# The softmax shift taken from the first 8 keys of a head instead of the first 16

## The chip, the cores and the metric

The kernel runs on one core of a Trainium2 chip. The metric is the device time of one execution in microseconds (us); the time of a kernel is the median of its runs. One execution is also recorded by the hardware profiler, and the profile and the trace are of that one.

## What is computed

Two branches of the same input `x` (2048 tokens of 448) are mixed by a gate `g` per token. Branch A is attention with 16 heads of 28, whose heads share one set of keys and values. Branch B is a layer norm, a token shift and an MLP of width 1792.

```python
q = (x @ wq) -> 16 heads of 28;  k = x @ wk;  v = x @ wv      # one k and v for all heads
scores = einsum("bhqd,bkd->bhqk", q, k) * 28 ** -0.5
p = softmax(scores)                                            # over 2048 keys
a = einsum("bhqk,bkd->bhqd", p, v) -> 448 columns @ wo
hs = shift(gelu(layernorm(x) @ w1)) @ w2;  x1 = x + hs
b = x1 + gelu(layernorm(x1) @ w3) @ w4
out = g * a + (1 - g) * b
```

A softmax is the same for any shift that is subtracted from all scores of a query, as long as nothing overflows or vanishes.

## The kernel before

The work is in three stages, each in an order that is written out by hand for every engine (nothing is rescheduled). Matmuls of stages 1 and 2 are made in three products of a high and a low part each.

- Stage 1 (to about 125 us): queries, keys and values of all tokens (`proj`, L133 to L139), the first layer norm, `w1` (`h`), `w2` (`hs`).
- Stage 2 (to about 397 us): the MLP in four blocks of 512 tokens. Each block has 14 tiles `g`: 11 products with `w3` (L135 to L139, moving operands `ah` and `al`), two GELUs on ACT (L689, L690), the low part on DVE (L691), then 3 products with `w4` for each of 4 token tiles (L699 to L701). `w3` and `w4` come in seven sets `w3h`, `w3l`, `w4h`, `w4l`; the first three sets lie in one pool (`s2a`), the other four in another.
- Stage 3: attention, in 16 units. A unit `u` is 512 queries by 4 heads. It passes over 16 key tiles, two per iteration, so 8 iterations `i` per unit.

An iteration of stage 3 has, on PE, the scores of two key tiles (`scores`, L204; 4 heads side by side in 4 row strips), then the products with the values of the two key tiles of the iteration before (`values`, L893; 4 heads in 4 column strips, in two halves of 256 queries), and mostly one "job": a product with `wo` (L844). The trace shows each f32 product of L893 and L844 as two records. On ACT it has the exponentials (`exps`, L257). DVE copies a half of one key tile's scores out of its banks (L954), adds the values' products up (`values_end`, L818) and adds the job's result (L860).

The shift: subtracting it happens inside the score products, since two spare rows of the queries `qh` hold the negated shift and the same rows of the keys hold 1. It is an estimate, the maximum over the first `MK` keys. `khd` holds these keys in bf16, four times on a diagonal, so that one product gives all four heads at once: 32 queries, in one of 4 column strips, by `4 * MK` columns.

```python
for i, t in enumerate(ts):                       # max_products: 4 token tiles
    for c in range(4):                           # by 4 column strips
        ...
        nc.tensor.matmul(ps[32 * c:32 * c + 32, i * 4 * MK:(i + 1) * 4 * MK], q, khd,
                         start=True, stop=True, tile_position=(0, 32 * c))
...
nc.vector.reduce_max(mx_of[u][:, :, ts[0]:ts[0] + n].rearrange("p j t -> p t j"),     # max_reduce
                     ps[:, 0:n * 4 * MK].rearrange("p (t j k) -> p t j k", t=n, j=4), axis=AX.X)
```

`max_part` calls both (L211 and L218). For unit 0 this is done in stage 2, among the `w4` products. For every later unit it is done in the iteration `i == 2` of the unit before, between the two halves of the values' products, into a score bank that is free just then; the next iteration's scores write that bank again. One iteration later `max_end` (L246 to L254) negates the result, splits it into two parts, transposes it and sends it into the spare rows by DMA.

`khd` is filled on POOL in stage 2 (L734 clears it, L737 casts the keys in, four times). On POOL also stand the clears of a part of the weight sets `w3h` (L111, in stages 1 and 2).

Because the shift is only an estimate, the reciprocals of all sums are compared with `LIMIT = 1e18` and `1 / LIMIT` (`check`, L801). The flags are counted at the end (L1056, L1059); if one is not good, a general path follows (`redo`, from L1066): for all 16 units again, with `max_full`, the maximum over all keys.

Of the kernel before, what the change touches and what calls it, by code (L numbers as in the profile page):

```python
# [30 lines left out]
EPS = 1e-5  # L31
SHIFTS = (-1, 1, -2, 2)
PB = 5
MK = 16
LIMIT = 1e18


def f32(ap):
    return ap.bitcast(F32)
# [3 lines left out]
def gated_mix_kernel(  # L43
# [162 lines left out]
    def max_products(u, ts, ps):  # L206
        for i, t in enumerate(ts):
            for c in range(4):
                m = t * P + 32 * c
                q = f32(qh_of[u])[:, m:m + 32].bitcast(BF16).rearrange("p (m e) -> p m e", e=2)[:, :, 1]  # L210
                nc.tensor.matmul(ps[32 * c:32 * c + 32, i * 4 * MK:(i + 1) * 4 * MK], q, khd,  # L211
                                 start=True, stop=True, tile_position=(0, 32 * c))

    def max_reduce(u, ts, ps):
        if u not in mx_of:
            mx_of[u] = late.tile([P, 4, 4], F32, tag="mr", bufs=2, name=f"mr_{u}")
        n = len(ts)
        nc.vector.reduce_max(mx_of[u][:, :, ts[0]:ts[0] + n].rearrange("p j t -> p t j"),  # L218
                             ps[:, 0:n * 4 * MK].rearrange("p (t j k) -> p t j k", t=n, j=4), axis=AX.X)

# [41 lines left out]
    with tc.tile_pool(name="s1b", bufs=1) as s1b, \  # L262
# [325 lines left out]
        late = ctx.enter_context(tc.tile_pool(name="late", bufs=1, side="right", reuse_waits="tile"))  # L588
        khd = late.tile([P, 4 * MK], BF16, name="khd")
        kh_of.append(late.tile([P, S], F32R, name="kh"))  # L590
# [76 lines left out]
    with tc.tile_pool(name="s2", bufs=1, reuse_waits="tile") as s2, \  # L667
# [35 lines left out]
        for b in range(NB):  # L703
            acc = [ps2.tile([P, 512], F32, tag="acc", bufs=4, name=f"acc_{b}_{t}") for t in range(4)]
            gs = {}
            for f in range(NF):
# [26 lines left out]
                if b == 1 and f == 1:  # L733
                    nc.gpsimd.memset(khd, 0.0)  # L734
                    for j in range(4):
                        h = slice(32 * j, 32 * j + DH)
                        nc.gpsimd.tensor_copy(khd[h, j * MK:(j + 1) * MK], f32(kh_of[0])[h, 0:MK])  # L737
                    qr0 = s2a.tile([P, 512], F32, tag="xn", bufs=1, name="qr_0")
# [406 lines left out]
```

## Time and profile before

| | |
|---|---|
| median of 3 runs | 911.8 us (911.51 to 913.12) |
| the profiled execution | 911.48 us |
| its span, first to last instruction | 909.7 us |
| busy: PE, ACT, DVE, POOL | 903.1, 632.6, 515.8, 79.1 us |
| granted TensorE clock, mean | 0.999 |

In the profile PE is TensorE's matmuls and PEld its weight loads, which run beside the matmuls; DVE is VectorE, ACT ScalarE, POOL GpSimd and SP the engine that issues most DMAs. A row of a group reads: line, engine, operation, output <- inputs, output <- input shape, number | busy us, mean ns of one | idle time before it. A row of the timeline reads: start us, length us, engine, line, operation, and in brackets the idle time before it and what ended it. L12 is line 12 of the kernel.

### The profile page before, as it was taken

The numbers are of one execution on the slowest core, as the hardware profiler recorded it, in microseconds if no ns is written. First come the engines' busy times: TensorE is split into PE (matmuls) and PEld (weight loads), VectorE is DVE, ScalarE is ACT, GpSimd is POOL, SyncE is SP. The second block draws the span as 40 slices with busy tenths as digits, with TensorE's granted clock in tenths as the row PEclk, the third lists the DMA queues.
The fourth block names the chain that finished last, engine by engine and source line by source line (L and its number), as shares of the span: only waits on it lengthen the run. The fifth ranks groups of instructions, "written<-read, shape, count | busy, mean of one in ns | idle before, by whom it ended". The sixth has DMA issues, their size and how long they took to land.

```text
span 909.7 us, 24149 instructions
## 1 busy us (share of the span) xinstructions
PE 903.1 (99%) x10360; PEld 626.8 (69%) x10360; DVE 515.8 (57%) x960; ACT 632.6 (70%) x1003; POOL 79.1 (9%) x116
## 2 busy tenths in 40 slices
PE   9999999999999999999999999999999999999998
PEld 6788888888888888875555555555555555555554
DVE  3665273631441531136766777676767667767665
ACT  5542444332132231269999999999999999999995
POOL 3243320200000520020000000000000000000000
PEclk9999999999999999999999999999999999999999
DMA  8832653120110120010000001000011000010001
GB/s 294 289 103 61 147 167 129 37 70 1 39 49 2 22 65 1 1 52 24 14 25 14 24 15 56 23 25 17 25 33 36 24 14 25 15 55 14 15 14 44
DMA packets 40726, 47.31 MB, mean 52 GB/s; under 512 B 10152, under 2 KB 28904, under 8 KB 40616
## 3 DMA queue, kind: packets, MB, share of 16 engines
q1 hardware_dynamic: 37448, 40.43, 15.2%
q10 hardware_dynamic: 3168, 5.31, 1.6%
q8 instruction: 82, 1.34, 0.6%
q14 instruction: 28, 0.23, 0.1%
HBM read 32.56 MB, written 11.67 MB: 49 GB/s over the span
## 4 chain that ended last, share of the span: by engine, by line
PE 97%; ACT 2%; DMA 1%; DVE 0%; issue 0%; SPq 0%
PE bank L893 26%; PE bank L204 20%; PE bank L844 6%; PE acc L701 5%; PE acc L699 5%; PE acc L700 5%; PE g L135 4%; PE g L137 4%; PE g L136 4%; PE pair L204 2%; ACT p L257 2%; PE hs L475 1%; PE hs L476 1%; PE g L138 1%; PE g L139 1%; PE h L136 1%
## 5 line engine op out<-in xcount | busy, mean ns | idle before, releaser
L257 ACT ACTIVATE p<-bank 128x512 f32<-128x512 f32 x514 | 265.9, 605 | 4.4 <-POOL pick L866 1.5
L893 PE MATMUL bank<-p,vext 128*32 128x256 f32 x4064 | 247.7, 382 | 1.0 <-ACT p L257 1.0
L893 PEld LDWEIGHTS bank<-p,vext 128*32 128x32 f32 x4064 | 117.9, 110 | 115.9 <-ACT p L257 53.0
L954 DVE COPY p<-pair 128x1024 f32<-128x1024 f32 x125 | 153.0, 1224 | 57.9 <-PE pair L204 40.9
L689 ACT ACTIVATE gh<-g 128x512 fp32r<-128x512 f32 x55 | 32.9, 598 | 181.7 <-PE g L139 181.7
L818 DVE TENSOR_TENSOR o<-o,bank 128x256 f32<-128x256 f32 x222 | 93.5, 421 | 80.4 <-PE bank L893 72.3
L257 ACT ACTIVATE p<-p 128x1024 f32<-128x1024 f32 x126 | 138.0, 1096 | 0.0
L257 ACT ACTIVATE p<-pair 128x1024 f32<-128x1024 f32 x129 | 136.8, 1060 | 0.0
L691 DVE TENSOR_TENSOR gl<-gf,gh 128x512 fp32r<-128x512 f32 x55 | 38.6, 702 | 164.9 <-ACT gf L690 164.9
L204 PE MATMUL bank<-qh,kh 32*128 32x512 f32 x514 | 114.8, 443 | 0.0
L204 PE MATMUL pair<-qh,kh 32*128 32x512 f32 x510 | 114.0, 443 | 0.0
L204 PE MATMUL bank<-qh,kl 32*128 32x512 f32 x514 | 101.8, 389 | 0.0
L204 PE MATMUL bank<-ql,kh 32*128 32x512 f32 x514 | 101.6, 390 | 0.0
L204 PE MATMUL pair<-qh,kl 32*128 32x512 f32 x510 | 101.3, 389 | 0.0
L204 PE MATMUL pair<-ql,kh 32*128 32x512 f32 x510 | 100.9, 389 | 0.0
L204 PEld LDWEIGHTS bank<-qh,kh 32*128 32x128 f32 x514 | 48.0, 182 | 61.3 <-issue 38.7
L701 PE MATMUL acc<-w4h,gl 128*128 128x448 f32 x220 | 80.7, 367 | 0.0
L699 PE MATMUL acc<-w4h,gh 128*128 128x448 f32 x220 | 80.2, 364 | 0.0
L700 PE MATMUL acc<-w4l,gh 128*128 128x448 f32 x220 | 79.8, 363 | 0.0
L844 PE MATMUL bank<-wof,on 128*32 128x224 f32 (+1 forms) x984 | 69.6, 357 | 0.0
L135 PE MATMUL g<-ah,w3h 128*128 128x512 f32 x168 | 65.4, 389 | 0.0
L136 PE MATMUL g<-al,w3h 128*128 128x512 f32 x168 | 65.4, 389 | 0.0
(206 smaller groups left out, 1394.1 us busy)
## 6 DMA issues: line engine op xcount, KB each, us to landing
qd<-qf ACTq DMA_DIRECT2D x15, 256.0 KB
rb<-rd SPq DMA_DIRECT2D x15, 256.0 KB
x<-in_x_dram SPq DMA_DIRECT2D x4, 896.0 KB
xd<-xt SPq DMA_DIRECT2D x16, 224.0 KB
w34raw<-in_w_dram SPq DMA_DIRECT2D x7, 512.0 KB
qr<-qd SPq DMA_DIRECT2D x64, 56.0 KB
w34raw<-in_w_dram SPq DMA_DIRECT2D x7, 448.0 KB
out_dram<-ot SPq DMA_DIRECT2D x14, 224.0 KB
```

The source lines that it names most:

```text
L135: nc.tensor.matmul(ps, wh[:, c, :], ah[:, c, :], start=(c == 0), stop=False)
L136: nc.tensor.matmul(ps, wh[:, c, :], al[:, c, :], start=False, stop=False)
L204: nc.tensor.matmul(ps[j], k[h, keys], q[h, :], start=(r == 0), stop=(r == 2), tile_position=(32 * j, 0))
L257: nc.scalar.activation(p[:, heads], p[:, heads] if source is None else source, AF.Exp, scale=SCALE)
L691: nc.vector.tensor_sub(gl, gf, f32(gh))
L699: nc.tensor.matmul(ps, gh[:, tok], w4h[i][:, k, :], start=(f == 0), stop=False)
L700: nc.tensor.matmul(ps, gh[:, tok], w4l[i][:, k, :], start=False, stop=False)
L701: nc.tensor.matmul(ps, gl[:, tok], w4h[i][:, k, :], start=False, stop=(f == stop))
L818: nc.vector.tensor_add(o, o, pv)
L844: nc.tensor.matmul(ps[32 * i:32 * i + 32, :], a[:, c:c + 32], w, start=start, stop=stop, tile_position=(0, 32 * i))
L893: nc.tensor.matmul(pv[32 * j:32 * j + 32, :], vext[:, kt, :], p_of[k][:, j, qs], start=(k == ks[0]), stop=(k == ks[-1]), tile_position=(0, ...
L954: nc.vector.tensor_copy(pa[:, both], pairs[0])
```

## The change

One constant:

```diff
-MK = 16
+MK = 8
```

`khd` becomes 128x32 instead of 128x64, the products of L211 have 32 columns instead of 64, the reduction of L218 reads 128 elements per partition instead of 256 (16 groups of 8 instead of 16), and the casts of L737 take 8 keys instead of 16. The general path with all keys stays.

No instruction is added, removed or moved on any engine. On PE, at the `w4` products of stage 2 where the estimate for unit 0 stands (`m` is its PSUM tile, `acc` that of the `w4` products), the order reads, in part:

```order
 L701 MATMUL acc_0_2293<-w4h_1068,gl_0_2310 128x448
 L211 LDWEIGHTS qh_1048
-L211 MATMUL m_2354<-khd,qh_1048 32x64
+L211 MATMUL m_2354<-khd,qh_1048 32x32
 L211 LDWEIGHTS qh_1048
```

All 256 products change in this way, and each keeps its own load of weights. On POOL, at the clears of `w3h` at the end of stage 1 and at the filling of `khd` in stage 2, with the semaphores that each instruction waits for:

```order
 L111 MEMSET w3h_0_1066 64x256 [waits PE_49,Pool_49]
-L111 MEMSET w3h_1_1186 64x256 [waits PE_49]
+L111 MEMSET w3h_1_1186 64x256
 L111 MEMSET w3h_2_1229 64x256
 L111 MEMSET w3h_3_1295 64x256 [waits DMAHW5_49,DMAHW4_49,PE_49]
...
-L734 MEMSET khd_1046 128x64
-L737 CAST khd_1046<-kh_1047 28x16 [waits Pool_49]
+L734 MEMSET khd_1046 128x32
+L737 CAST khd_1046<-kh_1047 28x8 [waits Pool_49]
 L739 MEMSET qr_0_1848 128x512 [waits DVE_49,Pool_49]
```

The second clear no longer waits for PE: `khd` takes 64 bytes less per partition, the buffers that are allocated below it (the pools `bigs` and `s2a`: raw inputs, `ah`, `al`, the first three weight sets and small statistics tiles) lie 64 bytes higher, and one of them no longer touches a buffer of stage 1 that PE still reads. All other waits are the same.

## The prediction, made before the changed kernel ran

> **What bounds the kernel now.** I read the page first: the busy shares, then the chain that ended last.
>
> ```profile
> PE 903.1 (99%) x10360; PEld 626.8 (69%) x10360; DVE 515.8 (57%) x960; ACT 632.6 (70%) x1003; POOL 79.1 (9%) x116
> PE 97%; ACT 2%; DMA 1%; DVE 0%; issue 0%; SPq 0%
> ```
>
> TensorE is in use for nearly the whole span and carries 97% of the chain. The shares are averages, so next come the stages. The estimate of the maximum (products at L211, reduction at L218) is made once in stage 2 and fifteen times in stage 3. Two views of one line each, the instructions of L211 and those of L218:
>
> ```profile
> L211 PEld LDWEIGHTS <-qh x256: 91/97/98, 270.6 to 845.0; 128*32 128x32 bf16 x128
> L211 PE MATMUL pair<-khd,qh x240: 192/193/194, 408.1 to 845.1; 128*32 128x64 bf16 x120
> L211 PE MATMUL m<-khd,qh x16: 192/193/204, 270.6 to 270.7; 128*32 128x64 bf16 x16
> L218 DVE TENSOR_REDUCE mr<-pair x15: 418/421/421, 408.7 to 845.6; 128x16 f32<-128x256 f32 x15
> ```
>
> So there are 16 blocks of 16 products. Those of stage 3 lie one unit apart, about 31.2 us ((845.1 - 408.1) / 14), at 408, 439, 470 and so on to 845 us. In stage 3 two engines are nearly full, and it has to be told which sets the pace. The table by windows (columns: window, length, then busy us and instructions of PE, PEld, DVE, ACT, POOL, then clock and DMA), the waits of ACT from 445 to 880 us, and the head of the chain from 414 to 446 us:
>
> ```profile
> 445.00:900.00 455.00, 455.00 (x7678) 257.87 (x7673) 319.28 (x602) 451.76 (x697) 0.00 (x0) 1.00 0.08 24
> ACT p L257 <- PE pair L204: 0.4, 1, 0.4
> by line: ACT p L257 44.4%; PE bank L893 25.4%; PE bank L204 21.6%; PE bank L844 4.7%; issue 2.7%; PE pair L204 1.8%
> ```
>
> From 445 us PE has no gap at all, at full clock. ACT is close behind. Before 446 us, where iterations with and without an output job alternate, ACT is the largest part of the chain. The chain in order of time around one block (start, us, what) settles the later stretch:
>
> ```profile
> 465.14 1.91 PE bank L893 x32
> 467.05 0.38 PE bank L844 x8
> 467.43 0.42 PE bank L204
> ...
> 469.03 1.05 PE bank L893 x16
> 470.08 0.12 PE pair L211 x16
> 470.20 0.87 PE bank L893 x16
> 471.06 0.38 PE bank L844 x8
> 471.44 0.43 PE bank L204 x2
> ...
> 475.33 0.43 PE bank L204 x2
> ```
>
> Nothing but PE stands in it. From one start of the scores to the next it is 471.44 - 467.43 = 4.01 us with the block in between, and 475.33 - 471.44 = 3.89 us without. The difference, 0.12 us, is the block's own row. In this stretch the block is therefore paid in full, once per unit.
>
> **The change part by part.**
>
> *The products, 256 of them, from 64 columns to 32.* Their number, their weights and their place stay. Thirteen blocks (470 to 845 us) lie where PE paces, two (408 and 439 us) where ACT does, and one in stage 2. In the thirteen a block costs 0.12 us, that is 4 turns of the four column strips at 30 ns. Two things could set the 30 ns. If it is the columns that stream, half of them take half the time: 0.06 us saved per block. If it is the rate at which loads and products follow one another, nothing much is saved. The block of stage 2 shows that rate, since its 16 loads run without older work in front (timeline; start, us, engine, line):
>
> ```profile
> 270.33 0.37 PE L701 MATMUL acc<-w4h,gl 128*128 128x448 f32 x1
> 270.62 0.18 PEld L211 LDWEIGHTS <-qh 128*32 128x32 bf16 x16 [0.31 <-issue]
> 270.62 0.30 PE L211 MATMUL m<-khd,qh 128*32 128x64 bf16 x16
> 270.86 0.19 PEld L699 LDWEIGHTS acc<-w4h,gh 128*128 128x128 f32 x1
> ```
>
> Sixteen loads of 97 ns fit in 0.18 us, so one follows another after (180 - 97) / 15 = 5.5 ns; sixteen products of 193 ns fit in 0.30 us, which is (300 - 193) / 15 = 7.1 ns each. Sixteen pairs need 0.09 to 0.11 us at this rate, whatever their width, against the 0.12 us now. That leaves 0.01 to 0.03 us per block. I take 0.015 us, since the measured rate of the products (7.1 ns) is nearer to the block's own (120 / 16 = 7.5 ns) than to half of it. Thirteen blocks: 0.2 us; if the columns set it, 13 x 0.06 = 0.8 us; the whole block gone would be 13 x 0.12 = 1.6 us, a bound that nothing can reach while the loads stay.
>
> The Trainium skill speaks against the larger sum: TensorE: Matmul & The Clock Gate, section "Wait — 56ns, not 53.3ns?", says that start to start never drops below about 25 ns however few the columns are. Applied to each of the four turns of a block, that rule would leave an estimated 30 - 25 = 5 ns per turn, 0.02 us per block and 0.26 us for the thirteen. The trace shows no product of 32 columns, so it neither bears the floor out nor denies it; the 30 ns of a turn at 64 columns lie above it.
>
> In the two ACT-paced blocks PE has time to spare, so I count nothing; by the streaming price they would bring at most 2 x 0.06 us. The one of stage 2 stands on the path of a PE-paced stage too, with its first load exposed (0.31 us idle): 0.015 us by the issue rate, 0.06 us at most, and the exposed load stays.
>
> *The reduction, 16 times from 256 to 128 elements.* The nearest rows are the present one, 420 ns, and a narrow one on the same engine:
>
> ```profile
> L246 DVE TENSOR_SCALAR mc<-mr 128x16 fp32r<-128x16 f32 x13 | 2.1, 165 | 0.0
> 470.20 0.42 DVE L818 TENSOR_TENSOR o<-o,bank 128x256 f32<-128x256 f32 x1 [0.55 <-PE bank L893]
> 470.54 0.42 DVE L218 TENSOR_REDUCE mr<-pair 128x16 f32<-128x256 f32 x1
> 471.19 0.42 DVE L818 TENSOR_TENSOR o<-o,bank 128x256 f32<-128x256 f32 x1 [0.23 <-issue]
> ```
>
> (420 - 165) / 240 = 1.06 ns per element, so an estimated 0.14 us less each time and 2.2 us in all. I cost it at nothing, because the next L818 starts 0.23 us after the reduction has ended: it waits for the second half of L893 on PE, not for DVE. The next scores overwrite the reduced bank only at 471.44, half a microsecond after 470.96, with the job's products (0.38 us) between. In the two early blocks no job lies between, but there ACT paces. If that cover were gone, up to 0.14 us per block would come on top.
>
> *POOL: a narrower clear and four narrower casts of the key copy, and one wait less.* The timeline of POOL:
>
> ```profile
> 118.80 0.81 POOL L111 MEMSET w3h<- 64x256 f32 x3
> 124.88 0.82 POOL L111 MEMSET w3h<- 64x256 f32 x3 [5.27 <-PE hs L478]
> ...
> 171.36 0.16 POOL L734 MEMSET khd<- 128x64 bf16 x1
> 171.58 1.01 POOL L737 CAST khd<-kh 28x16 bf16<-28x16 f32 x4
> 176.78 0.53 POOL L739 MEMSET qr<- 128x512 f32 x1 [4.19 <-DVE xt L164]
> ```
>
> The wait that goes belongs to the second of the six clears, which ran inside the first three without a gap: it was met already. The 5.27 us belong to the fourth, whose wait stays. The casts, 1.01 us, end 4.19 us before POOL's next work can start, and their first reader comes at 270.6 us. Nothing to gain or lose.
>
> *A shift of addresses.* The key copy takes 64 bytes less per partition, so the allocator puts the buffers of stage 2 that lie below it 64 bytes higher: ah and al (moving in all w3 products), the first three of seven weight sets, and the raw buffers. The trace has no column for addresses; I bound the cost by rows whose tiles stand at both offsets. In the built program the tiles of stage 1 lie at offset 96 modulo 128, those of stage 2 at 32 before and at 96 (or still at 32) after. Groups by form, of 120 to 400 us and of 20 to 95 us:
>
> ```profile
> L135 PE MATMUL g<-ah,w3h 128*128 128x512 f32 x168 | 65.4, 389 | 0.0
> L135 PE MATMUL h<-ahk,w1h 128*112 128x512 f32 x36 | 14.2, 396 | 0.0
> L139 PE MATMUL q<-ahk,wql 128*128 128x512 f32 x10 | 3.9, 389 | 0.0
> ```
>
> At offset 96 the same product took 389 ns in one group and 396 in another, in a stage with more traffic. I take the 389, which is the quieter group with weights of the same width: no cost. The ends are nothing and 7 ns on each of 616 w3 products (56 sets of 11), 4.3 us.
>
> *The sum.* -0.2 us on a span of 909.7 us and a profiled execution of 911.48 us, so 909.5 and 911.3. The median of the runs shown is 911.8, 0.3 above the profiled one; the forecast for the median is 911.8 - 0.2 = 911.6 us. A change of 0.2%, 1.8 us, is about what a measurement of this kernel can tell from none, so this is the middle class.
>
> **The rivals.**
>
> *Faster: DVE turns out to pace the blocks.* If the release of the bank by L218 were what PE waits for, the 0.14 us of each of 15 reductions would come through beside the 0.06 us of the products: 15 x 0.2 = 3.0 us, 908.8 us. For it speaks that the early blocks have the next scores right behind the reduction; against it that PE shows no gap from 445 us. To pass 1.8 us it needs 0.12 us in every block. I give this, and other gains of that size, 0.12.
>
> *Slower: the moved buffers make the w3 products dearer.* Price 7 ns x 616 = 4.3 us by the row of 396 ns: 915.9 us. It decides from 1.8 / 616 = 3 ns a product on. For it: one group at the new offset is that slow, and stage 2 is PE-bound, so each ns counts. Against it: two groups at the two offsets both take 389 ns. 0.10.
>
> *Slower by far: the general path runs.* A shift from 8 keys is lower, so sums of exponentials grow; past 1e18 the kernel repeats the attention with a maximum over all keys. Worked out from the reference's inputs by the kernel's formula, the largest logarithm of a sum over the shift goes from 25.1 (16 keys) to 30.0 (8 keys), the least stays at 0.1; the limit is ln 1e18 = 41.4. Were it to run, the scores, exponentials and values alone would come again, at least 16 units x 8 iterations x 3.89 us = 498 us: over 1,400 us. 0.02.
>
> *The change doesn't act at all* (a block stays at 0.12 us): 911.8 us, inside the forecast's class, 0.3 of its 0.76.
>
> **How the numbers follow.** Forecast 0.76 (gain between 0 and 0.8 us), faster 0.12, slower 0.10 + 0.02 = 0.12. The range starts from 911.8 - 0.8 = 911.0 and from the spread of the runs, 911.51 to 913.12 (0.3 below the median, 1.3 above it). That gives 911.0 - 0.3 = 910.7 and 911.8 + 1.3 = 913.1; with some of both rivals, 910.4 to 913.2.
>
> **What would show it right or wrong.** Right: the L211 row of the chain between 0.09 and 0.12 us, 16 blocks as before, L218 near 0.28 us with the wait of L818 behind it longer by as much, 3.89 us per iteration, 389 ns for w3 products, and no instruction from the general path. Streaming would show as an L211 row of 0.06 us. Wrong: another mean for L135 to L139 or L699 to L701, ACT idle in stage 3, an iteration after a block that is shorter than 3.89 us, or instructions behind the last output's store.

## The result and the profile after

| | before | after |
|---|---|---|
| median of 16 runs each | 911.83 us (911.39 to 913.12) | 913.72 us (913.26 to 914.3) |
| the profiled execution | 911.48 us | 913.26 us |
| its span | 909.7 us | 911.4 us |

The changed kernel is slower: after over before is 1.0019, with a 95% interval from 1.0013 to 1.0026, or 1.9 us. The forecast was 911.6 us, a gain of 0.2 us that can hardly be told from none, and 913.72 lies above the top of its range, 913.2.

The page of the kernel after, first its span and busy shares, then the shares of the chain that ended last:

```profile
span 911.4 us, 24149 instructions
PE 905.2 (99%) x10360; PEld 626.2 (69%) x10360; DVE 513.3 (56%) x960; ACT 632.4 (69%) x1003; POOL 79.2 (9%) x116
PE 97%; ACT 2%; DVE 0%; DMA 0%; issue 0%; DVEq 0%
```

The counts are the same as before, so no general path ran. DVE is busy 2.5 us less. PE is busy 2.1 us more, and PE is 97% of the chain.

The instructions that the change makes smaller, L211 and L218 in the kernel after (number, then shortest/median/longest in ns):

```profile
L211 PEld LDWEIGHTS <-qh x256: 92/94/98, 271.4 to 846.8; 128*32 128x32 bf16 x128
L211 PE MATMUL pair<-khd,qh x240: 175/176/193, 409.9 to 846.9; 128*32 128x32 bf16 x120
L218 DVE TENSOR_REDUCE mr<-pair x15: 283/286/288, 410.5 to 847.4; 128x16 f32<-128x128 f32 x15
```

A product takes 176 ns instead of 193, a reduction 286 instead of 421. All starts of stage 3 lie later than before: the first block of that stage at 409.9 instead of 408.1, the last at 846.9 instead of 845.1. The delay is 1.8 us at both ends, so it came about before stage 3 and stays constant in it.

The chain in order of time around the block near 472 us, in the kernel after, shows the block itself:

```profile
465.38 0.43 PE bank L204 x2
469.27 0.43 PE bank L204 x2
470.88 1.03 PE bank L893 x16
471.92 0.10 PE pair L211 x15
472.01 0.88 PE bank L893 x16
472.89 0.38 PE bank L844 x8
473.27 0.42 PE bank L204 x2
```

It stands at 0.10 us, before at 0.12. From scores to scores it is 473.27 - 469.27 = 4.00 us with the block (before 4.01), and 469.27 - 465.38 = 3.89 without (before 3.89).

So the time was lost earlier. The timeline has two marks that bound stage 2: its first `w3` product, and the first scores of stage 3. Before:

```profile
124.66 0.39 PE L135 MATMUL g<-ah,w3h 128*128 128x512 f32 x1
395.88 0.51 PE L204 MATMUL bank<-qh,kh 32*128 32x512 f32 x4
```

After:

```profile
124.51 0.39 PE L135 MATMUL g<-ah,w3h 128*128 128x512 f32 x1
397.59 0.50 PE L204 MATMUL bank<-qh,kh 32*128 32x512 f32 x4
```

Stage 2 lasts 397.59 - 124.51 = 273.08 us instead of 395.88 - 124.66 = 271.22. That is 1.86 us more, the whole of the loss. From the second mark to the end of the span it is 513.8 us in both.

In stage 2 PE is never idle (busy 271.22 of 271.22 us before, 273.08 of 273.08 after), so the 1.86 us must lie in the products. Their groups by form from 120 to 400 us (number | busy us, mean ns | idle) are, for two lines of before (the third, L135, stands in the prediction):

```profile
L136 PE MATMUL g<-al,w3h 128*128 128x512 f32 x168 | 65.4, 389 | 0.0
L137 PE MATMUL g<-ah,w3l 128*128 128x512 f32 x168 | 65.4, 389 | 0.0
```

and after:

```profile
L137 PE MATMUL g<-ah,w3l 128*128 128x512 f32 x168 | 66.0, 393 | 0.0
L135 PE MATMUL g<-ah,w3h 128*128 128x512 f32 x168 | 65.7, 391 | 0.0
L136 PE MATMUL g<-al,w3h 128*128 128x512 f32 x168 | 65.7, 391 | 0.0
```

The `w3` products became 2 to 4 ns longer, although the change doesn't touch them. Products overlap, so what counts is the time from one start to the next. One tile `g` with the sixth weight set, its first (L135) and last (L139) of 11 products, before:

```profile
307.22 0.39 PE L135 MATMUL g<-ah,w3h 128*128 128x512 f32 x1
309.49 0.39 PE L139 MATMUL g<-ah,w3l 128*128 128x512 f32 x1
```

and after:

```profile
308.26 0.39 PE L135 MATMUL g<-ah,w3h 128*128 128x512 f32 x1
310.56 0.40 PE L139 MATMUL g<-ah,w3l 128*128 128x512 f32 x1
```

Ten steps take 2.27 us before and 2.30 after: 227 and 230 ns. Over all tiles, from the starts in the trace at full resolution, the mean step went from 226.6 to 227.9 ns with the first three weight sets, and from 226.6 to 230.3 with the last four; the step of the `w4` products with the first three sets went from 203.0 to 203.8. Four blocks of 14 tiles are 264, 352 and 288 products: 264 x 1.3 + 352 x 3.7 + 288 x 0.8 ns = 1.88 us, against 1.86 measured.

### The profile page after: what moved, and what is told of

The parts are those of the page before. It is cut to its first block, busy times and chain, and to the rows that moved or that the text cites. A ratio compares the mean times of both kernels' runs of the same rounds, so it can differ in the third digit from the quotient of the medians.

```text
span 911.4 us, 24149 instructions
## 1 busy us (share of the span) xinstructions
PE 905.2 (99%) x10360; PEld 626.2 (69%) x10360; DVE 513.3 (56%) x960; ACT 632.4 (69%) x1003; POOL 79.2 (9%) x116
## 4 chain that ended last, share of the span: by engine, by line
PE 97%; ACT 2%; DVE 0%; DMA 0%; issue 0%; DVEq 0%
PE bank L893 26%; PE bank L204 19%; PE bank L844 6%; PE acc L699 5%; PE acc L701 5%; PE acc L700 5%; PE g L137 4%; PE g L136 4%; PE g L135 4%; PE pair L204 2%; ACT p L257 2%; PE hs L475 1%; PE hs L476 1%; PE g L139 1%; PE g L138 1%; PE h L136 1%
## 5 line engine op out<-in xcount | busy, mean ns | idle before, releaser
L137 PE MATMUL g<-ah,w3l 128*128 128x512 f32 x168 | 66.0, 393 | 0.0
L135 PE MATMUL g<-ah,w3h 128*128 128x512 f32 x168 | 65.7, 391 | 0.0
```

Of the source, the lines that this page charges most:

```text
L135: nc.tensor.matmul(ps, wh[:, c, :], ah[:, c, :], start=(c == 0), stop=False)
L137: nc.tensor.matmul(ps, wl[:, c, :], ah[:, c, :], start=False, stop=False)
```

## The experiments

The theory (A): the changed addresses did it. `khd` shrank by 64 bytes per partition, and what is allocated below it moved. The rival (B): the narrower estimate itself costs the time. Within A it was then asked what counts in an address: that `ah` and `al` stand at one offset (A2), that both operands of a product have the same offset modulo 128 (A1), or the distance between the two operands modulo 256 (A3). "Distance" below is the address of the moving operand less that of the product's weights, modulo 256 bytes, from the addresses in the built programs: `ah`, `al` less `w3h`, `w3l`, and `w4h`, `w4l` less `gh`, `gl`. Two unused spaces move buffers: columns added to `khd` move all that lies below it (`ah`, `al`, weight sets 0 to 2), and the kernel's spacer `gap2` in `s2` moves sets 3 to 6.

The table gives for each run its time, the ratio to the kernel before on the same chip, the length of stage 2 between the two marks, and distance : mean step in ns. Every edit but the number of keys is a move of addresses only. POOL's wait follows from the addresses: it is gone in after and e3, and there in all other runs. The `w4` column of sets 0 to 2 includes two steps of about 300 ns beside the L211 block of stage 2, 0.7 ns of its mean, so its numbers are compared within the column.

| run | us | ratio (95%) | stage 2 | w3, sets 0-2 | w3, sets 3-6 | w4, sets 0-2 | w4, sets 3-6 |
|---|---|---|---|---|---|---|---|
| before | 911.83 | | 271.22 | 0: 226.6 | 0: 226.6 | 192: 203.0 | 192: 202.3 |
| after | 913.72 | 1.0019 (1.0013 to 1.0026) | 273.08 | 0: 227.9 | 64: 230.3 | 0: 203.8 | 192: 202.4 |
| e1_mk8_pad | 911.48 | 1.0000 (0.9991 to 1.0009) | 271.20 | 0: 226.6 | 0: 226.6 | 192: 203 | 192: 202.3 |
| e2_mk16_shift | 914.93 | 1.0035 (1.0021 to 1.0049) | 274.42 | 0: 228.9 | 192: 232.7 | 128: 204.7 | 192: 202.1 |
| e3_mk8_gap64 | 912.75 | 1.0013 (1.0004 to 1.0023) | 272.19 | 0: 227.6 | 0: 228.0 | 0: 203.3 | 0: 202.6 |
| e4_mk16_gap64 | 914.52 | 1.0028 (1.0016 to 1.0039) | 273.84 | 0: 226.8 | 192: 233.2 | 192: 203.1 | 0: 202.9 |
| e5_mk4_pad | 911.71 | 1.0001 (0.9991 to 1.0010) | 271.19 | 0: 226.6 | 0: 226.6 | as before | as before |
| e6_all0 | 913.59 | 1.0018 (1.0009 to 1.0027) | 273.39 | 0: 226.9 | 0: 226.8 | 160: 205.9 | 160: 205.7 |
| e7_all64 | 912.07 | 1.0005 (0.9996 to 1.0014) | 271.96 | 0: 227.3 | 0: 227.4 | 224: 203.3 | 224: 202.8 |
| e8_mk16_gap56 | 914.70 | 1.0033 (1.0022 to 1.0044) | 274.28 | 0: 226.6 | 224: 232.8 | 192: 203.1 | 224: 204.6 |
| e9_mk8_gh32 | 914.51 | 1.0029 (1.0017 to 1.0040) | 274.19 | 0: 228.8 | 0: 229.9 | 128: 204.9 | 128: 204.3 |
| e10_mk16_shift128 | 913.29 | 1.0018 (1.0009 to 1.0027) | 272.79 | 0: 227.0 | 128: 232.4 | 64: 201.0 | 192: 202.3 |
| e11_mk8_gh96 | 910.40 | 0.9985 (0.9976 to 0.9994) | 269.81 | 0: 226.8 | 0: 226.6 | 64: 200.8 | 64: 200.3 |
| e12_mk16_shift512 | 912.06 | 1.0001 (0.9991 to 1.0010) | 271.22 | 0: 226.6 | 0: 226.5 | 192 | 192: 202.3 |
| e13_mk16_shift1024 | 911.56 | 0.9997 (0.9987 to 1.0006) | 271.20 | 0: 226.6 | 0: 226.6 | 192 | 192: 202.3 |
| e14_mk16_shift256 | 911.82 | 0.9997 (0.9988 to 1.0006) | 271.22 | 0: 226.6 | 0: 226.5 | 192 | 192: 202.3 |

**The addresses or the keys: e1 and e2.** e1 keeps the 8 keys and gives `khd` its old size; e2 keeps 16 keys and makes `khd` larger by 64 bytes.

```diff
 MK = 8        # e1;  MK = 16 in e2
-khd = late.tile([P, 4 * MK], BF16, name="khd")
+khd = late.tile([P, 64], BF16, name="khd")[:, 0:4 * MK]     # e1
+khd = late.tile([P, 96], BF16, name="khd")[:, 0:4 * MK]     # e2
```

> The change with the key copy kept at its old 128 bytes per partition (half unused), so every buffer stands where it stood before. Theory A (addresses): stage 2 gets its old times back, L135 to L139 389 ns each, and what is left of the change is the shorter block: 13 blocks of stage 3 by 0.0125 us, about 911.6 us, 0.2 below before; L211 blocks 0.103 to 0.104 us from first product to the next work. Theory B (the narrower estimate itself costs, through the order in which work follows): 913.7 us as with the change.

> Before, with 16 keys, and 64 unused bytes per partition added to the key copy: ah, al and the first three weight sets stand 64 bytes lower than before, at offset 96 modulo 128 as with the change, the blocks of the estimate as before. Theory A: about 913.7 us (+1.9), w3 products at 391 to 393 ns. Theory B: 911.8 us and 389 ns. If the absolute place matters and not the offset modulo 128, something between or outside the two.

The groups of e1 from 120 to 400 us:

```profile
L136 PE MATMUL g<-al,w3h 128*128 128x512 f32 x168 | 65.4, 389 | 0.0
L135 PE MATMUL g<-ah,w3h 128*128 128x512 f32 x168 | 65.4, 389 | 0.0
L137 PE MATMUL g<-ah,w3l 128*128 128x512 f32 x168 | 65.4, 389 | 0.0
```

With 8 keys and the old addresses the products are back at 389 ns, stage 2 at 271.20 us and the time at the level of before. With 16 keys and moved addresses it is 3.1 us slower than before. Theory B falls: all of the loss goes with the addresses. The wait on POOL is there in e2 too, so the loss doesn't come from its absence.

**Which address: e3 and e4.** Both move only weight sets 3 to 6 up by 64 bytes, e3 in the kernel after and e4 in the kernel before.

```diff
-s2.tile([P, 48], F32, name="gap2")
+s2.tile([P, 64], F32, name="gap2")
```

> The change, with the gap ahead of weight sets 3 to 6 made 64 bytes wider, so that all seven sets and ah and al stand at offset 96 modulo 128. Theory A1 (a product is slower where moving tile and weights stand at different offsets): the four sets fall from 230.3 ns start to start to about 228, 0.8 to 1.0 us back: 912.8 us. Theory A2 (slower because ah and al stand at 96, whatever the weights): no change, 913.7 us. If the match is all that counts, as before: 911.6 us.

> Before, with 16 keys and the same wider gap: weight sets 3 to 6 at offset 96, all else at 32 as before. Theory A1 (different offsets are slow): products of sets 3 to 6 go from 226.6 to about 230 ns, 352 x 3.7 ns = 1.3 us, 913.1 us. Theory A2 (the offset of ah and al counts): 911.8 us.

The groups of e4:

```profile
L136 PE MATMUL g<-al,w3h 128*128 128x512 f32 x168 | 66.0, 393 | 0.0
L137 PE MATMUL g<-ah,w3l 128*128 128x512 f32 x168 | 66.0, 393 | 0.0
L135 PE MATMUL g<-ah,w3h 128*128 128x512 f32 x168 | 65.9, 392 | 0.0
```

In e4 `ah` and `al` stand where they stood before, and the products with the moved sets still rise to 233.2 ns a step; those with sets 0 to 2 stay at 226.8. In e3 `ah` and `al` stand where the change put them, and moving the sets after them brings the step from 230.3 to 228.0. So it isn't the place of `ah` and `al` alone (A2 falls): the two operands have to be looked at together. e3 returns half of the loss only, 912.75 us; 1.0 to 1.4 ns a step remain with both operands moved alike.

**The size of the estimate alone: e5.** With `khd` at its old size, 4 keys instead of 8: products of 16 columns, a reduction of 64 elements.

```diff
-MK = 16
+MK = 4
-khd = late.tile([P, 4 * MK], BF16, name="khd")
+khd = late.tile([P, 64], BF16, name="khd")[:, 0:4 * MK]
```

> 4 keys (products of 16 columns, reduction of 64 elements), the key copy kept at its old 128 bytes, so all buffers as before. It tells what the floor of a block is. If the rate at which loads and products follow one another sets it, a block stays at 0.104 us as with 8 keys (0.116 with 16). If there is still a part that streams, it falls on, to about 0.09 us (another 0.0125). In time either is too small to tell: 911.4 to 911.8 us.

The instructions of L211 in e5, and the block near 470 us in its chain:

```profile
L211 PE MATMUL pair<-khd,qh x240: 169/169/173, 407.8 to 844.7; 128*32 128x16 bf16 x120
469.80 0.10 PE pair L211 x15
```

A product is shorter again, 169 ns, but the block stays at 0.10 us. At full resolution its 16 pairs of a load and a product take 0.116 us with 64 columns, 0.104 with 32, and 0.103 to 0.105 with 16: at 32 columns and fewer the rate of the pairs, 6.5 ns each, sets the block.

**Alike offsets: e6, e7, e8.** e6 and e7 (8 keys) bring both `w3` operands to offset 0 and to offset 64 modulo 128; e8 (16 keys) moves sets 3 to 6 by 32 bytes only.

```diff
+khd = late.tile([P, 80], ...)[:, 0:4 * MK];  s2.tile([P, 40], F32, name="gap2")    # e6
+khd = late.tile([P, 48], ...)[:, 0:4 * MK];  s2.tile([P, 56], F32, name="gap2")    # e7
+s2.tile([P, 56], F32, name="gap2")                                                 # e8
```

> 8 keys, with ah, al and all seven weight sets at offset 0 modulo 128 (key copy at 160 bytes, gap ahead of sets 3 to 6 at 160). Theory A1 (a mismatch is what costs): matched, so 226.6 to 227.8 ns start to start, 911.5 to 912.8 us. If a start on a multiple of 64 bytes also helps, fewer: 215 ns would be 512 columns at 2.4 per ns, 7 us less. If the offset itself counts (96 matched was 1.25 ns dearer than 32 matched), a third value.

> The same with all at offset 64 modulo 128 (key copy at 96 bytes, gap at 224). Theory A1: matched, 911.5 to 912.8 us; the pair of this run and the one at 0 shows whether the distance to 32 or 96 matters among matched ones.

> 16 keys, all as before but weight sets 3 to 6 at offset 64 (gap 32 bytes wider instead of 64). With 64 bytes the products of these sets cost 6.6 ns more, 2.7 us. If any mismatch costs the same: 233 ns, 914.5 us. If it grows with the distance: about 230 ns, 913.1 us. If only half a 128-byte line apart costs: 226.6 ns, 911.8 us.

With distance 0 the `w3` step is 226.8 to 227.4 ns at either offset; 32 bytes off, in e8, it is 232.8. e6 is nevertheless 2.0 us slower, and there it is the `w4` products: their operands came to distance 160, and the step went from 202.3 or 203.0 to 205.7 or 205.9, about 3 ns on 672 products, 2.0 us. So the `w4` products show the effect too, with another best distance.

**Modulo what: e10, e14, e12, e13.** In the kernel before, `khd` is made larger by 128, 256, 512 and 1024 bytes.

```diff
+khd = late.tile([P, 128], BF16, name="khd")[:, 0:4 * MK]    # e10; 192 in e14, 320 in e12, 576 in e13
```

> Before, 16 keys, with 128 unused bytes added to the key copy: ah, al and the first three weight sets stand 128 bytes lower, at the same offset 32 modulo 128 as before; sets 3 to 6 stay. If the offset modulo 128 is what counts: 226.6 ns start to start in all w3 products, 911.7 us. If the distance of the buffers as such, or a longer period, counts: 230 to 233 ns in some sets, 913 to 915 us.

> 16 keys, ah, al and the first three weight sets 512 bytes lower than before (448 unused bytes more at the key copy than in the run with 128), sets 3 to 6 as before. Before, all distances from ah and al to the seven weight sets are multiples of 1024 bytes; a shift of 32, 64 or 128 in that distance cost 4 to 7 ns per product, a common shift cost 0 to 1.3. Theory A3 (what counts is that distance, with a period of 512 or less): sets 3 to 6 at 226.6 to 227 ns, 911.8 us. If the period is longer: about 232 ns, 913.3 to 915 us.

> The same, 1024 bytes lower. Theory A3 with a period up to 1024: 226.6 ns, 911.8 us. If sets 3 to 6 stay at 232 ns (913.3 to 915 us), no period of the distance up to 1024 explains it, and that the two groups moved against each other at all is what counts.

> The same, 256 bytes lower. Theory A3 with a period of 256: 226.6 ns, 911.8 us; with one of 512 or 1024: 230 to 233 ns, 913.3 to 915 us.

The first and the last `w3` product of one tile with the sixth set, in e10:

```profile
308.23 0.40 PE L135 MATMUL g<-ah,w3h 128*128 128x512 f32 x1
310.56 0.40 PE L139 MATMUL g<-ah,w3l 128*128 128x512 f32 x1
```

and in e14:

```profile
307.81 0.39 PE L135 MATMUL g<-ah,w3h 128*128 128x512 f32 x1
310.08 0.39 PE L139 MATMUL g<-ah,w3l 128*128 128x512 f32 x1
```

Ten steps take 2.33 us after a shift of 128 bytes, and 2.27, as before, after a shift of 256. The offsets modulo 128 are the same in e10 as before, so A1 falls. 256, 512 and 1024 bytes leave stage 2 at 271.20 to 271.22 us. The distance modulo 256 (A3) accounts for these four runs and for e4.

**Moving the other pair: e9 and e11.** From e1, with `w3` at distance 0, a spacer `gap1` ahead of `gh` and `gl` moves these two up; `gap2` is made smaller by as much, so that sets 3 to 6 stay.

```diff
+s2.tile([P, 16], F32, name="gap1")     # e9;  [P, 32] in e11
-s2.tile([P, 48], F32, name="gap2")
+s2.tile([P, 32], F32, name="gap2")     # e9;  [P, 16] in e11
```

> 8 keys, all buffers as before, but gh and gl (the weights of the w4 products) 64 bytes higher, at offset 32 instead of 96, so that they match w4h and w4l. If a match is always the better, the w4 products fall from 202.6 ns start to start towards 199 to 201: 650 x 2 ns = 1.3 us, 910.3 us, which would beat both kernels. If the rule is one of the w3 products alone: 202.6 ns and 911.5 us. Dearer is open too: with w4h at 96 against gh at 96, matched, they took 203.0.

> 8 keys, all buffers as before, but gh and gl 128 bytes higher, so that w4h and w4l lie 64 bytes past a multiple of 1024 from them instead of 192. In the run with the 128-byte shift the first three sets stood so, and their products took 200.1 to 200.7 ns start to start for sets 1 and 2 against 202.3. Theory A3 for the w4 products too: 650 x 2 ns = 1.3 us less, 910.2 us, which would beat both kernels. If gh and gl against ah matter as well (with gh and gl 64 bytes higher, w3 cost 3 ns more): 911.5 to 914 us.

The `w4` products (by form, 120 to 400 us) before:

```profile
L701 PE MATMUL acc<-w4h,gl 128*128 128x448 f32 x220 | 80.7, 367 | 0.0
L700 PE MATMUL acc<-w4l,gh 128*128 128x448 f32 x220 | 79.8, 363 | 0.0
```

and the same two in e11, where their lines are 703 and 702:

```profile
L703 PE MATMUL acc<-w4h,gl 128*128 128x448 f32 x220 | 79.9, 363 | 0.0
L702 PE MATMUL acc<-w4l,gh 128*128 128x448 f32 x220 | 79.2, 360 | 0.0
```

At distance 64 the step is 200.3 to 200.8 ns instead of 202.3 to 203.0: about 2.1 ns on 672 products, 1.4 us, and stage 2 is 1.41 us shorter (269.81). e11 at 910.40 us (909.95 to 911.16) is faster than both kernels; its ratio to before lies below 1 with its whole interval. e9, at distance 128, made the `w4` step 2 ns dearer. It also made the `w3` step 2 to 3 ns dearer, although the `w3` operands did not move against each other. The distance of a product's own two operands doesn't explain that.

**What stays open.** Why the distance counts, whether by banks or by ports of the memory, no run shows. Three remainders don't follow from the distance: the `w3` step of e9 at distance 0 (228.8 and 229.9 ns), that of e3 and e7 (0.7 to 1.4 ns), and that of after and e2 with sets 0 to 2 (1.3 and 2.3 ns). The traces show where they lie, though not why: where PE changes between `w4` and `w3` products. In after, e2, e3 and e9 a tile that follows another `w3` tile keeps, on average, 226.0 to 227.2 ns in each of its first ten steps. In e9, a tile of sets 3 to 6, which follows `w4` products, takes 228 to 236 ns in its first six steps, 226.5 to 226.9 in the next four and 232.6 in its last, up to the start of `w4`. In e7 only that last step is long, 235 ns.

The 230.3 ns of after at distance 64 is also a mean over unlike steps, from 227.0 to 234.0 by the place in the tile; at 128, 192 and 224 (e2, e4, e8, e10) no place falls below 229.1. One rival wasn't tested: in these traces the load of a product's weights starts about 223 ns before the product, just after the product before it has started. What clashes could therefore be a moving operand and the weights of the next product. Within a tile these stand at the same distance modulo 256 as the product's own two operands, so the runs don't separate the two.

## Why the prediction was wrong, point by point

- **The products of the estimate: right.** Their number and place stay, and the block fell from 0.116 to 0.104 us, 0.012 each, where 0.015 was taken and streaming would have given 0.06. The one in stage 2 fell from 0.232 to 0.205, 0.027 where 0.015 was taken. e5 confirms the reason, since half the columns once more changed nothing. On the floor of 25 ns from start to start that the Trainium skill gives (TensorE: Matmul & The Clock Gate, "Wait — 56ns, not 53.3ns?"), the runs agree if it is applied to a turn of four strips: a turn went from 29 to 26 ns and with 16 columns stayed at 26. For single products in column strips it does not hold: they follow every 6.5 ns.
- **Their sum, 0.2 us: neither seen nor denied.** 13 x 0.012 is 0.16 us. Stage 3 with 16 keys took 513.8 to 514.3 us over eight profiled executions, with 8 keys 513.6 to 514.2 over seven: more spread than the gain. e1, which differs from before in the keys alone, has a ratio of 1.0000 with an interval of 0.0009 either way.
- **The reduction: right.** 0.135 us less each time (421 to 286 ns; 0.14 predicted) and nothing of it in the time. In the timeline of the kernel after, the addition behind it still waits, and for longer, 0.35 us instead of 0.23:

```profile
472.38 0.28 DVE L218 TENSOR_REDUCE mr<-pair 128x16 f32<-128x128 f32 x1
473.01 0.42 DVE L818 TENSOR_TENSOR o<-o,bank 128x256 f32<-128x256 f32 x1 [0.35 <-issue]
```

- **POOL and the wait that went: right.** No part of the loss is left for them, since the products account for all 1.86 us (1.88 by the sum of the steps), and e2 and e4 lose more with the wait in place.
- **A shift of addresses: this step failed.** It had the right place (the `w3` products of stage 2), but took "no cost". Its evidence was one quiet group of stage 1 at offset 96 that ran at 389 ns. That group could not show the effect: in the `proj` products of stage 1 both operands stood at a distance that is a multiple of 256, as those of `w3` did in stage 2 before. The step asked where the buffers stand, and should have asked where the two operands stand to each other. The shift moved `ah` and `al` with weight sets 0 to 2, but not with sets 3 to 6; that only three of seven sets move stands in the prediction itself and was not used. Nor do all tiles of stage 2 lie at 32, as the step has it: `gh` and `gl` lie at 96, and the `w4` products were not priced. Its other end was mis-sized: 7 ns on 616 products, 4.3 us, against 1.3 ns on 264 and 3.7 on 352, 1.6 us, and 0.23 us in the `w4` products. The 1.3 ns, 0.3 us in all, stand at distance 0 and belong to the remainders above. The row of 396 ns behind the 7 ns also stood at a multiple of 256, so the distance doesn't explain it, and no run shows what does.
- **The rival "the moved buffers make the w3 products dearer": right in place and direction, with 4.3 us instead of 1.6.** Its reason, the offset 96 by itself, was not right: e4 is slow with `ah` and `al` at 32. It was to decide from 3 ns a product; 1.6 us on 616 is 2.7, just below that point, and the `w4` products brought the rest. The sign named beforehand, another mean for L135 to L139, is the one that showed. The three other rivals did not occur.
- **The range.** It was said to hold "some of both rivals", and one of them was priced at 4.3 us. Its top, 913.2, came from the spread of the runs before with 0.1 us added, so hardly any of that price was in it. With half of the price the top would have been 911.8 + 2.1 = 913.9.

## What to carry to other kernels

A change of a buffer's size is a change of every address behind it. Before a small gain is forecast, list from the built program which operands of the products that pace the kernel move against each other, and price that move on all of those products: here 0.2 us stood against 1.9. Giving the shrunken buffer its old size separates the two in one run, and a spacer put ahead of one operand can then bring a gain of its own (e11, 910.40 us).

## What was unexpected of the hardware

The step of the f32 products of stage 2, with TensorE full, goes with the distance of their two operands in memory modulo 256 bytes. For the 128x512 products of `w3` it was 226.6 ns at distance 0 in the old placement, 230.3 at 64, and 232.4 to 233.2 at 128, 192 and 224. Other moves alone brought it at distance 0 to between 226.6 and 229.9, by the changes between `w4` and `w3`. For the 128x448 products of `w4` the least was 200.3 to 201.0 ns at 64, then 202.1 to 203.8 at 192 and 0, 202.8 to 204.9 at 224 and 128, and 205.7 to 205.9 at 160. Shifts by 256, 512 and 1024 bytes changed nothing. In this kernel the placement alone is worth from 910.4 to 914.9 us.
